# Attention tiles taken in pairs in a one-core attention, soft-MoE and SwiGLU kernel

## The chip, the cores and the metric

The kernel runs on one core of a Trainium2 chip, in one launch. Its time is device microseconds of that core; the times shown are medians of several runs. One more execution was recorded by the hardware profiler, and all durations below come from that one.

## The reference

Three stages follow each other. Eight batches with eight heads of 576 positions and 64 channels go through attention in chunks of 64 positions; the result, 4608 tokens of 512 channels, goes through a soft mixture of experts (8 experts, 4 slots each, hidden size 1024) and then through a gated feed-forward layer of 1536 channels.

```python
q_c, k_c, v_c = (a.reshape(B, H, nc, 64, D) for a in (q, k, v))
scores = scale * np.matmul(q_c, k_c.transpose(0, 1, 2, 4, 3))
attn = np.exp(scores - scores.max(-1, keepdims=True))
x = np.matmul(attn / (attn.sum(-1, keepdims=True) + 1e-9), v_c)   # as [4608, 512]
logits = x @ phi                                                  # 32 slots
d = softmax over tokens; slot_input = d.T @ x
slot_out[e] = relu(slot_input[e] @ w1[e]) @ w2[e]
y = softmax over slots of logits @ slot_out
out = (silu(y @ w_gate) * (y @ w_val)) @ w_out
```

q, k, v, phi, w1 and w2 are float32. The three weights of the last layer are float64, and the kernel turns them into pairs of float32 on the chip.

## The kernel before, in words

**Attention.** The 4608 tokens are 36 tiles of 128 (NTILE), each with 8 heads, which stand as 4 pairs of heads (j) and 2 chunks of 64 positions (cc). For tile i:

- load_qk (L293) and load_v (L296) bring q, k (512 KB) and v with a column of ones (260 KB) from HBM. Each has a ring of three buffers (NK, NV), qkbd and vbd. A load waits until the tile three before has been used: q and k by emit_scores, v by emit_pv.
- spread_k and spread_v (L321, L322) make the buffer block-diagonal: a copy of its lower 64 partitions to another place, and a memset of what they leave. They run on POOL (the first spread_k on DVE).
- emit_scores (L337): 8 small float32 matmuls into PSUM; then on DVE the row maximum (L345) and its subtraction (L347) into ssb.
- emit_pt (L359): 4 transposes of ssb against the identity, and an Exp on ACT (L361), which writes pt.
- emit_pv (L399): 8 matmuls with v, each with 130 columns, into two PSUM banks; the 65th column of each head is the row sum. DVE adds 1e-9 (L407), takes the reciprocal (L408) and multiplies (L410) into x_sb.
- emit_xt (L423): 4 transposes of x_sb, copied by ACT (L425).
- Every fourth tile, for a group g of four tiles: emit_logits (16 matmuls with phi, a running maximum, an Exp), then emit_et (one transpose of the group's weights) and emit_si (4 matmuls of 512 columns that gather the slots' inputs).

The compiler records each float32 matmul of 64 or 32 columns as two instructions in the profile, so that 8 matmuls stand there as x16.

A program order written out by hand sets what each engine does when. Each engine takes its instructions in that order and stops at one that waits. The loop (L548 to L572) for tile i is:

```python
emit_pt(i); emit_scores(i + 2); load_qk(i + 5); spread_v(i + 1); spread_k(i + 3)
emit_et; emit_xt(i - 1); emit_pv(i); load_v(i + 3); emit_logits; emit_si
if i % 2: pump(1)
```

**Weights.** All loads are issued by one queue, SP, in program order. pump takes the next entry of the list lq when one of 16 slots of 8 KB a partition (pool wp) is free: w1t and w2t are halves of an expert's weights, 1 MB each. In the attention loop it takes one entry for every two tiles; 16 halves are loaded in that way, and 4 more go into a pool (wx) that takes the place of the rings at the end. The first quarter of the gate and value weights (raw, load_gv0) is converted in steps (conv_a, conv_b, conv_c) during the attention loop, with scratch in a pool cv1.

**Experts.** emit_w1 and emit_w2 go through the experts in a fixed order; each half that has been used frees a slot (freed), and pump issues the next load.

**Feed-forward.** From L913 on the token blocks go through gate, value and output matmuls in fp32r, in an order set by SCHED; each product is split into a high and a low part (hi_sb, lo_sb), and the output takes three matmuls of 512 columns for each 128 tokens and 128 channels (L889 to L891). The output goes to HBM from SP.

**Memory.** Pools on the left side of SBUF lie one behind the other in the order in which they are opened: const, sm (small vectors, three buffers each), wp, and then those of the attention (atp, xp, xtp, cv1), whose place c_t and others take afterwards. PSUM has 8 banks: in the attention two for scores (ps_s), two for emit_pv (ps_x) and four (ps_t) for everything else.

Of the kernel before, what the change touches and what calls it, by code (L numbers as in the profile page):

```python
# [25 lines left out]
LATE = 3  # L26
C_AT = (3, 4, 5, 6, 7, 9, 10, 11, 12)
# [6 lines left out]
def tile_attn_softmoe_swiglu(  # L34
# [26 lines left out]
    cvp = [None]  # L61
    wp = ctx.enter_context(tc.tile_pool(name="wp", bufs=NW))
# [70 lines left out]
    lq = [(load_gv0, 0)]  # L133
# [42 lines left out]
    def conv_a():  # L176
# [6 lines left out]
        if c == 0 and kind != "o" and u == 1:  # L183
            i = "gv".index(kind)
            mt = tmp_t[0][:, i * 512:(i + 1) * 512]
            ex = tmp_t[0][:, 1024 + i * 256:1280 + i * 256].bitcast(U16)
        else:
            ex = cv.tile([128, 512], U16, tag="ex", name="ex", bufs=1 if cv is cv1 else 3)
            mt = cv.tile([128, 512], I32, tag="mt", name="mt")
# [13 lines left out]
    def conv_c():  # L203
# [4 lines left out]
        if c == 0 and kind != "o":  # L208
# [4 lines left out]
            if kind == "v":  # L213
                if u == 0:
                    freed(load_gv0, 0)
                else:
                    freed(alloc_tmp)
# [56 lines left out]
    with tc.manual_schedule():  # L274
        p1 = ExitStack()
        atp = p1.enter_context(tc.tile_pool(name="atp", bufs=2))
        xp = p1.enter_context(tc.tile_pool(name="xp", bufs=6))
        xtp = p1.enter_context(tc.tile_pool(name="xtp", bufs=4))
        cv1 = cvp[0] = p1.enter_context(tc.tile_pool(name="cv1", bufs=1))
        ps_s = p1.enter_context(tc.tile_pool(name="ps_s", bufs=2, space=PSUM))  # L280
        ps_x = p1.enter_context(tc.tile_pool(name="ps_x", bufs=1, space=PSUM))
        ps_t = p1.enter_context(tc.tile_pool(name="ps_t", bufs=4, space=PSUM))
# [83 lines left out]
        def emit_pv_last(i):  # L366
            pt = pt_t.pop(i)
            x = xp.tile([128, 2, 4, D], F32, tag="x", name="x_sb")
            rec = sm.tile([128, 2, 4, 1], F32, tag="rec", name="rec")
            xvs = []  # L370
            for b in range(2):
                xps = ps_s.tile([128, 512], F32, tag="s", name="x_ps")
                for j in (2 * b, 2 * b + 1):
                    for cc in range(2):
                        nc.tensor.matmul(
                            out=xps[64 * cc:64 * cc + 64, (j % 2) * 2 * VW:(j % 2 + 1) * 2 * VW],
                            lhsT=pt[:, j, 64 * cc:64 * cc + 64],
                            rhs=v_bd[i % NV][:, :, cc, j, :],
                            start=True, stop=True,
                        )  # L380
                xvs.append(xps[:, 0:4 * VW].rearrange("p (h d) -> p h d", d=VW))
            for b in range(2):
                nc.vector.tensor_scalar(
                    out=rec[:, b], in0=xvs[b][:, :, D:VW], scalar1=1e-9, scalar2=None, op0=ALU.add
                )
            for b in range(2):
                nc.vector.reciprocal(out=rec[:, b], in_=rec[:, b])
            for b in range(2):
                nc.vector.tensor_tensor(
                    out=x[:, b], in0=xvs[b][:, :, 0:D], in1=rec[:, b].to_broadcast([128, 4, D]), op=ALU.mult  # L390
                )
            x_t[i] = x.rearrange("p b h d -> p (b h d)")

        def emit_pv(i):
            pt = pt_t.pop(i)
            xps = ps_x.tile([128, 2, 512], F32, tag="x", name="x_ps")
            for j in range(4):
                for cc in range(2):
                    nc.tensor.matmul(  # L399
                        out=xps[64 * cc:64 * cc + 64, j // 2, (j % 2) * 2 * VW:(j % 2 + 1) * 2 * VW],  # L400
                        lhsT=pt[:, j, 64 * cc:64 * cc + 64],
                        rhs=v_bd[i % NV][:, :, cc, j, :],
                        start=True, stop=True,
                    )
            xv = xps[:, :, 0:4 * VW].rearrange("p b (h d) -> p b h d", d=VW)
            rec = sm.tile([128, 2, 4, 1], F32, tag="rec", name="rec")
            nc.vector.tensor_scalar(out=rec, in0=xv[:, :, :, D:VW], scalar1=1e-9, scalar2=None, op0=ALU.add)  # L407
            nc.vector.reciprocal(out=rec, in_=rec)  # L408
            x = xp.tile([128, 2, 4, D], F32, tag="x", name="x_sb")
            nc.vector.tensor_tensor(  # L410
                out=x, in0=xv[:, :, :, 0:D], in1=rec.to_broadcast([128, 2, 4, D]), op=ALU.mult
            )
            x_t[i] = x.rearrange("p b h d -> p (b h d)")
# [21 lines left out]
        def emit_logits(g, jts=(0, 1, 2, 3), done=True):  # L435
# [21 lines left out]
            et = atp.tile([128, 128], F32, tag="et", name="et")  # L457
# [14 lines left out]
        def emit_et(g):  # L472
# [3 lines left out]
            e = atp.tile([128, 128], F32, tag="e", name="e")  # L476
# [64 lines left out]
        spread_k(1)  # L541
        spread_v(0)
        spread_k(2)
        emit_scores(0)
        load_qk(3)
        emit_scores(1)
        load_qk(4)
        for i in range(NTILE - 2):  # L548
            emit_pt(i)
            emit_scores(i + 2)  # L550
            if i + 2 + NK < NTILE:
                load_qk(i + 2 + NK)
            spread_v(i + 1)
            if i + 3 < NTILE:
                spread_k(i + 3)
            if i >= 5 and (i - 5) % 4 == 0:
                emit_et((i - 5) // 4)
            if i >= 1:
                emit_xt(i - 1)
            emit_pv(i)  # L560
            if i + NV < NTILE:
# [446 lines left out]
```

## Time and profile before

| what | value |
|---|---|
| median of 3 runs | 576.01 us (574.79 to 576.03) |
| the profiled execution's own time | 579.36 us |
| its span in the profile | 577.6 us |
| TensorE (PE) busy, share of the span | 547.5 us, 95% |
| DVE, ACT, POOL busy | 422.8, 264.7, 291.6 us |
| read from HBM, written | 80.95 MB, 9.44 MB |
| chain that ended last: PE, DMA, POOL, DVE | 77%, 10%, 5%, 4% |

The profile's time is in microseconds from the span's start. The attention loop runs from about 10 us to 151 us, the experts from 160 us to about 202 us, the feed-forward layer from there to the end. In a row of the page's issues the columns are the tensors (out, from where), the queue, the count, the size and the median time from issue to landing. In the chain each row has a start, a duration and what it was: the chain is followed back from the end, at each step to what released it. A busy PE is not a PE at its peak: each matmul's recorded time covers its way through the array, and several are under way at once; the distance from one block's first start to the next block's first start tells what a block costs. The granted TensorE clock is 1.00 (2.4 GHz) in all stretches.

### The profile page before, as it was taken

The numbers are of one execution on the slowest core, as the hardware profiler recorded it, in microseconds if no ns is written. First come the engines' busy times: TensorE is split into PE (matmuls) and PEld (weight loads), VectorE is DVE, ScalarE is ACT, GpSimd is POOL, SyncE is SP. The second block draws the span as 40 slices with busy tenths as digits, with TensorE's granted clock in tenths as the row PEclk, the third lists the DMA queues.
The fourth block names the chain that finished last, engine by engine and source line by source line (L and its number), as shares of the span: only waits on it lengthen the run. The fifth ranks groups of instructions, "written<-read, shape, count | busy, mean of one in ns | idle before, by whom it ended". The sixth has DMA issues, their size and how long they took to land.

```text
span 577.6 us, 10084 instructions
## 1 busy us (share of the span) xinstructions
PE 547.5 (95%) x3823; PEld 422.4 (73%) x3823; DVE 422.8 (73%) x748; ACT 264.7 (46%) x500; POOL 291.6 (50%) x322
## 2 busy tenths in 40 slices
PE   4999999989999977999999999999999999999997
PEld 3766776776743465788888878887888788888885
DVE  4778777767566489998889887997989764443464
ACT  1344333333334467666666555564555543333331
POOL 4557654554200136667566565763766463443432
PEclk9999999999999999999999999999999999999999
DMA  8898999998989990101120221023000000032145
GB/s 274 270 333 326 313 335 325 348 320 283 350 307 385 381 393 35 36 38 30 44 74 0 74 77 70 1 74 145 1 1 1 0 2 0 14 120 87 73 177 188
DMA packets 37967, 91.03 MB, mean 158 GB/s; under 512 B 3104, under 2 KB 5152, under 8 KB 37920
## 3 DMA queue, kind: packets, MB, share of 16 engines
q1 hardware_dynamic: 37920, 90.40, 44.1%
q8 instruction: 30, 0.49, 0.3%
q14 instruction: 17, 0.14, 0.1%
HBM read 80.95 MB, written 9.44 MB: 157 GB/s over the span
## 4 chain that ended last, share of the span: by engine, by line
PE 77%; DMA 10%; POOL 5%; DVE 4%; issue 2%; ACT 1%; SPq 0%; POOLq 0%; DVEq 0%; ACTq 0%
PE o L889 16%; PE o L891 16%; PE o L890 16%; DMA vbd<-in_v_dram 7%; PE v_ps L845 4%; PE s_ps L337 4%; PE g_ps L845 4%; PE x_ps L399 4%; PE h_ps L648 3%; DMA w2t<-in_moe_w_dram 2%; PE xt_ps L423 2%; PE gg_ps L826 2%; PE so_ps L693 1%; PE pt_ps L359 1%; PE si_ps L488 1%
## 5 line engine op out<-in xcount | busy, mean ns | idle before, releaser
L858 POOL TENSOR_TENSOR lo_sb<-s_sb,hi_sb 128x512 fp32r<-128x512 f32 x106 | 140.6, 1327 | 134.0 <-ACT hi_sb L857 130.8
L889 PE MATMUL o<-whl,hi_sb 128*128 128x512 f32 x428 | 167.4, 391 | 3.8 <-DVE part L898 3.8
L891 PE MATMUL o<-whl,lo_sb 128*128 128x512 f32 x428 | 166.8, 390 | 0.5 <-POOL lo_sb L858 0.5
L890 PE MATMUL o<-whl,hi_sb 128*128 128x512 f32 x428 | 166.7, 390 | 0.0
L848 ACT ACTIVATE s_sb<-g_ps 128x512 f32<-128x512 f32 (+1 forms) x110 | 64.7, 590 | 153.2 <-PE g_ps L845 151.0
L849 DVE TENSOR_TENSOR s_sb<-s_sb,v_ps 128x512 f32<-128x512 f32 (+1 forms) x110 | 73.9, 673 | 77.8 <-ACT s_sb L848 76.4
L889 PEld LDWEIGHTS o<-whl,hi_sb 128*128 128x128 f32 x428 | 80.3, 188 | 23.6 <-DVE part L898 5.9
L891 PEld LDWEIGHTS o<-whl,lo_sb 128*128 128x128 f32 x428 | 80.3, 188 | 17.7 <-POOL lo_sb L858 0.9
L890 PEld LDWEIGHTS o<-whl,hi_sb 128*128 128x128 f32 x428 | 80.4, 188 | 16.2
L857 ACT ACTIVATE hi_sb<-s_sb 128x512 fp32r<-128x512 f32 (+1 forms) x110 | 67.6, 616 | 0.8 <-DVE s_sb L849 0.8
L902 DVE TENSOR_TENSOR part<-part,o 128x512 f32<-128x512 f32 x92 | 57.0, 676 | 2.6 <-PE o L891 2.6
L337 PE MATMUL s_ps<-qkbd 128*64 128x128 f32 x576 | 42.0, 291 | 15.4 <-POOL qkbd L322 9.6
L219 POOL TENSOR_TENSOR mt<-mt,ex 128x512 f32<-128x512 f32 x32 | 39.5, 1234 | 30.6 <-PE g_ps L845 15.1
L337 PEld LDWEIGHTS s_ps<-qkbd 128*64 128x64 f32 x576 | 32.9, 144 | 22.4 <-POOL qkbd L322 12.4
L205 DVE SCALAR_TENSOR_TENSOR ex<-raw,ex 128x512 uint16<-128x512 uint16 x34 | 49.1, 1443 | 0.1
L321 POOL COPY vbd<-vbd 64x520 f32<-64x520 f32 x36 | 22.8, 632 | 48.9 <-DMA vbd<-in_v_dram 46.5
L845 PE MATMUL v_ps<-c_t,g_st 128*128 128x512 f32 (+1 forms) x110 | 42.6, 391 | 3.1 <-ACT s_sb L848 2.5
L345 DVE TENSOR_REDUCE m<-s_ps 128x8 f32<-128x512 f32 x36 | 24.8, 690 | 26.4 <-PE s_ps L337 26.4
L845 PE MATMUL g_ps<-c_t,g_st 128*128 128x512 f32 (+1 forms) x110 | 42.2, 386 | 0.1
L361 ACT ACTIVATE pt<-pt_ps 128x512 f32<-128x512 f32 x36 | 21.3, 594 | 45.8 <-PE pt_ps L359 45.8
L399 PE MATMUL x_ps<-vbd,pt 128*64 128x130 f32 x560 | 39.0, 280 | 0.0
L200 DVE SCALAR_TENSOR_TENSOR mt<-mt,raw 128x512 f32<-128x512 f32 x34 | 36.1, 1063 | 0.0
(144 smaller groups left out, 721.2 us busy)
## 6 DMA issues: line engine op xcount, KB each, us to landing
qkbd<-in_qk_dram SPq DMA_DIRECT2D x36, 512.0 KB, 5.9
w1t<-in_moe_w_dram SPq DMA_DIRECT2D x16, 1024.0 KB, 8.0
w2t<-in_moe_w_dram SPq DMA_DIRECT2D x15, 1024.0 KB, 10.6
vbd<-in_v_dram SPq DMA_DIRECT2D x36, 260.0 KB, 5.4
out_dram<-part SPq DMA_DIRECT2D x36, 256.0 KB, 2.1
raw<-in_moe_w_out_dram SPq DMA_DIRECT2D x6, 1024.0 KB, 7.6
raw<-in_moe_w_gate_dram SPq DMA_DIRECT2D x5, 1024.0 KB, 5.4
raw<-in_moe_w_val_dram SPq DMA_DIRECT2D x5, 1024.0 KB, 5.1
```

The costliest lines, as they stand in the source:

```text
L205: nc.vector.scalar_tensor_tensor(out=ex, in0=hh, scalar=0x8000, in1=ex, op0=ALU.bitwise_and, op1=ALU.bitwise_or)
L337: nc.tensor.matmul(out=sp[64 * cc:64 * cc + 64, j, :], lhsT=qk_bd[i % NK][:, 0, j, t0:t0 + 64], rhs=qk_bd[i % NK][:, 1:3, j, t0:t0 + 64], ...
L399: nc.tensor.matmul(out=xps[64 * cc:64 * cc + 64, j // 2, (j % 2) * 2 * VW:(j % 2 + 1) * 2 * VW], lhsT=pt[:, j, 64 * cc:64 * cc + 64], rhs= ...
L845: nc.tensor.matmul(out=ps[:, k], lhsT=g_st[:, c, gi, ff:ff + 128], rhs=c_blk(b)[:, k], start=True, stop=True)
L848: nc.scalar.activation(out=s[:, k], in_=gp[:, k], func=ACTF.Silu)
L849: nc.vector.tensor_tensor(out=s[:, k], in0=s[:, k], in1=vp[:, k], op=ALU.mult)
L857: nc.scalar.activation(out=hi[:, k], in_=s[:, k], func=ACTF.Copy)
L858: eng.tensor_tensor(out=lo[:, k], in0=s[:, k], in1=hi[:, k].bitcast(F32), op=ALU.subtract)
L889: nc.tensor.matmul(out=a, lhsT=hi[:, ts], rhs=w_hi, start=first, stop=False)
L890: nc.tensor.matmul(out=a, lhsT=hi[:, ts], rhs=w_lo, start=False, stop=False)
L891: nc.tensor.matmul(out=a, lhsT=lo[:, ts], rhs=w_hi, start=False, stop=last)
L902: nc.vector.tensor_tensor(out=p[:, t], in0=p[:, t], in1=a, op=ALU.add)
```

## The change

The attention loop takes two tiles per step. emit_pv takes a pair p (tiles 2p and 2p+1): its 16 matmuls fill three PSUM banks, with three products of 130 columns in a bank instead of two (xa has two banks, xb one), and the DVE work is done once for the 12 heads of xa and once for the 4 heads of xb, six instructions for two tiles as before. load_v for tiles 2p+3 and 2p+4 is called inside emit_pv, after each tile's matmuls. emit_pv_last goes. Scores, transposes and spreads of two tiles stand next to each other. PSUM is now 2 banks for scores, 3 for emit_pv and 3 for the rest (4 before).

The pool cv1 goes: the first conversions use a slot of wp as scratch (alloc_tmp at the head of lq), which is freed after the second one. xp has 4 buffers of two tiles instead of 6 of one, et and e one buffer each. The strip pad_l of 416 bytes opens the pool const; rec in the pool sm grows from 8 to 16 floats, three times, which is 96 bytes. Both together move wp and all that lies behind it on that side by 512 bytes; the constants behind the strip move by 416.

```diff
+    const.tile([128, 104], F32, name="pad_l")
...
-    lq = [(load_gv0, 0)]
+    lq = [(load_gv0, 0), (alloc_tmp,)]
...
-        if c == 0 and kind != "o" and u == 1:
+        if c == 0 and kind != "o":
...
-        xp = p1.enter_context(tc.tile_pool(name="xp", bufs=6))
+        xp = p1.enter_context(tc.tile_pool(name="xp", bufs=4))
-        cv1 = cvp[0] = p1.enter_context(tc.tile_pool(name="cv1", bufs=1))
-        ps_t = p1.enter_context(tc.tile_pool(name="ps_t", bufs=4, space=PSUM))
+        ps_t = p1.enter_context(tc.tile_pool(name="ps_t", bufs=3, space=PSUM))
...
+        def emit_pv(p):
+            xa = ps_x.tile([128, 2, 512], F32, tag="xa", name="xa_ps")
+            xb = ps_x.tile([128, 512], F32, tag="xb", name="xb_ps")
+            banks = [xa[:, 0], xa[:, 1], xb]
+            for n in range(8):
+                i, j = 2 * p + n // 4, n % 4
+                for cc in range(2):
                     nc.tensor.matmul(
+                        out=banks[n // 3][64 * cc:64 * cc + 64, (n % 3) * 2 * VW:(n % 3 + 1) * 2 * VW],
+                        lhsT=pt_t[i][:, j, 64 * cc:64 * cc + 64],
                         rhs=v_bd[i % NV][:, :, cc, j, :],
                         start=True, stop=True,
                     )
+                if j == 3:
+                    pt_t.pop(i)
+                    if i + NV < NTILE:
+                        load_v(i + NV)
...
-        for i in range(NTILE - 2):
-            emit_pt(i)
-            emit_scores(i + 2)
...
+        NP = NTILE // 2
+        for p in range(NP):
+            if p < NP - 1:
+                for i in (2 * p + 2, 2 * p + 3):
+                    emit_scores(i)
+                    if i + NK < NTILE:
+                        load_qk(i + NK)
+            emit_pv(p)
+            for i in range(2 * p + 2, min(2 * p + 4, NTILE)):
+                if i + 2 < NTILE:
+                    spread_k(i + 2)
+                spread_v(i)
+            if p >= 3 and p % 2:
+                emit_et((p - 3) // 2)
+            if p >= 1:
+                emit_xt(2 * p - 2)
+                emit_xt(2 * p - 1)
+            if p < NP - 1:
+                emit_pt(2 * p + 2)
+                emit_pt(2 * p + 3)
+            if p >= 2 and p % 2 == 0:
+                emit_logits(p // 2 - 1)
+            if p >= 3 and p % 2:
+                if p == NP - 1:
+                    emit_logits(NG - 1, (0, 1), False)
+                emit_si((p - 3) // 2)
+            pump(1)
+            conv_step(p >= CV_FROM and conv_pos() < 2 and not conv_busy())
```

**PE, four tiles in the middle of the loop.** Before (s_ps scores, pt_ps and xt_ps transposes, x_ps the products with v, lt_ps logits, e_ps and si_ps the group's work; qkbd and vbd are the rings; x4 and x8 are matmuls of one row):

```order
23 L359 MATMUL pt_ps<-ident,ssb 128x128 x4
24 L337 MATMUL s_ps<-qkbd_101 64x128 x8
25 L475 MATMUL e_ps<-ident,et 128x128
26 L423 MATMUL xt_ps<-ident,x_sb 128x128 x4
27 L399 MATMUL x_ps<-vbd_105,pt 64x130 x8
28 L488 MATMUL si_ps<-x_sb,e 32x512 x4
29 L359 MATMUL pt_ps<-ident,ssb 128x128 x4
30 L337 MATMUL s_ps<-qkbd_102 64x128 x8
31 L423 MATMUL xt_ps<-ident,x_sb 128x128 x4
32 L399 MATMUL x_ps<-vbd_103,pt 64x130 x8
33 L359 MATMUL pt_ps<-ident,ssb 128x128 x4
34 L337 MATMUL s_ps<-qkbd_100 64x128 x8
```

and now:

```order
23 L359 MATMUL pt_ps<-ident,ssb 128x128 x8
24 L428 MATMUL lt_ps<-xt,phi_sb 32x128 x16
25 L337 MATMUL s_ps<-qkbd_100 64x128 x8
26 L337 MATMUL s_ps<-qkbd_98 64x128 x8
27 L373 MATMUL xa_ps<-vbd_101,pt 64x130 x8
28 L373 MATMUL xa_ps<-vbd_102,pt 64x130 x4
29 L373 MATMUL xb_ps<-vbd_102,pt 64x130 x4
30 L462 MATMUL e_ps<-ident,et 128x128
31 L410 MATMUL xt_ps<-ident,x_sb 128x128 x8
32 L359 MATMUL pt_ps<-ident,ssb 128x128 x8
33 L475 MATMUL si_ps<-x_sb,e 32x512 x4
34 L337 MATMUL s_ps<-qkbd_99 64x128 x8
```

The shape changed 18 times in four tiles; it now changes 8 times, and the transposes of x_sb and of ssb stand in one run.

**SP, the load queue, two pairs in the middle of the loop.** Before:

```order
31 L293 DMA qkbd_101<-in_qk_dram 128x1024
32 L296 DMA vbd_105<-in_v_dram 128x520
33 L293 DMA qkbd_102<-in_qk_dram 128x1024
34 L296 DMA vbd_103<-in_v_dram 128x520
35 L88 DMA w1t<-in_moe_w_dram 128x2x1024
36 L293 DMA qkbd_100<-in_qk_dram 128x1024
```

and now:

```order
30 L293 DMA qkbd_99<-in_qk_dram 128x1024
31 L293 DMA qkbd_100<-in_qk_dram 128x1024
32 L296 DMA vbd_103<-in_v_dram 128x520
33 L296 DMA vbd_101<-in_v_dram 128x520
34 L90 DMA w1t<-in_moe_w_dram 128x2x1024
35 L293 DMA qkbd_98<-in_qk_dram 128x1024
```

The same five loads per pair, with both of q and k ahead of both of v. On POOL spreads of k and v alternate as before, and the four of a step now stand together (qkbd and vbd are the rings' buffers):

```order
52 L321 COPY qkbd_98<-qkbd_98 64x512
53 L322 MEMSET qkbd_98 64x512
54 L321 COPY vbd_102<-vbd_102 64x520
55 L322 MEMSET vbd_102 64x520
56 L321 COPY qkbd_99<-qkbd_99 64x512
57 L322 MEMSET qkbd_99 64x512
58 L321 COPY vbd_103<-vbd_103 64x520
59 L322 MEMSET vbd_103 64x520
```

These eight rows are one step of the new loop, for the tiles 2p+4, 2p+2, 2p+5 and 2p+3. Each copy waits for its own load, and what stands behind it on POOL waits with it, as before.

## Rows read from the trace of the kernel before

**Rows 1.** Busy time by stretch: attention, its steady part, experts, loads alone; first row columns.

```profile
core 0: us, PE busy (x) PEld busy (x) DVE busy (x) ACT busy (x) POOL busy (x), PEclk, DMA share, GB/s
14.80:148.90 134.10, 126.57 (x1676) 94.70 (x1672) 99.99 (x224) 49.14 (x103) 75.64 (x134) 1.00 0.92 318
...
64.06:144.08 80.02, 75.78 (x1006) 56.45 (x1006) 57.60 (x130) 27.68 (x60) 44.02 (x81) 1.00 0.93 322
...
160.30:198.50 38.20, 37.34 (x312) 14.28 (x312) 24.71 (x98) 17.29 (x36) 2.74 (x10) 1.00 0.97 352
170.00:190.00 20.00, 20.00 (x173) 8.33 (x166) 13.88 (x59) 8.85 (x21) 0.50 (x4) 1.00 1.05 383
```

**Rows 2.** Chain that ended last, one stall of the attention loop; start, duration, what.

```profile
79.56 1.09 PE s_ps L337 x16
...
85.57 1.06 PE x_ps L399 x16
86.65 6.61 DMA vbd<-in_v_dram
93.39 0.62 POOL vbd L321
94.06 0.53 POOL vbd L322
94.59 0.56 POOL qkbd L321
95.20 0.53 POOL qkbd L322
95.78 1.09 PE s_ps L337 x16
```

**Rows 3.** Timeline of PE, one tile without a stall; start, duration, line, operation.

```profile
18.09 1.11 PE L399 MATMUL x_ps<-vbd,pt 128*64 128x130 f32 x16
...
19.12 0.66 PE L359 MATMUL pt_ps<-ident,ssb 128*128 128x128 f32 x4
...
19.71 1.09 PE L337 MATMUL s_ps<-qkbd 128*64 128x128 f32 x16
...
20.74 0.66 PE L423 MATMUL xt_ps<-ident,x_sb 128*128 128x128 f32 x4
...
21.32 1.11 PE L399 MATMUL x_ps<-vbd,pt 128*64 128x130 f32 x16
...
22.36 0.66 PE L359 MATMUL pt_ps<-ident,ssb 128*128 128x128 f32 x4
```

**Rows 4.** Timeline of PE at the end of attention, where two blocks of one shape touch.

```profile
146.84 1.09 PE L359 MATMUL pt_ps<-ident,ssb 128*128 128x128 f32 x8
147.86 1.06 PE L488 MATMUL si_ps<-x_sb,e 128*32 128x512 f32 x8
148.85 1.11 PE L399 MATMUL x_ps<-vbd,pt 128*64 128x130 f32 x16
149.79 1.05 PE L375 MATMUL x_ps<-vbd,pt 128*64 128x130 f32 x16
```

**Rows 5.** Page, DMA issues: the three kinds of load in the attention loop.

```profile
qkbd<-in_qk_dram SPq DMA_DIRECT2D x36, 512.0 KB, 5.9
w1t<-in_moe_w_dram SPq DMA_DIRECT2D x16, 1024.0 KB, 8.0
...
vbd<-in_v_dram SPq DMA_DIRECT2D x36, 260.0 KB, 5.4
```

**Rows 6.** Groups by line, 60 to 140 us: busy, mean ns, idle before, releaser.

```profile
L337 PE MATMUL s_ps<-qkbd 128*64 128x128 f32 x320 | 22.1, 279 | 4.5 <-POOL qkbd L322 4.5
...
L425 ACT ACTIVATE xt<-xt_ps 128x512 f32<-128x512 f32 x20 | 11.9, 597 | 16.2 <-PE xt_ps L423 16.2
...
L441 PE MATMUL lt_ps<-xt,phi_sb 128*32 128x128 f32 x160 | 5.4, 276 | 0.0
```

**Rows 7.** Chain that ended last, experts: their first matmuls and the last load.

```profile
160.31 1.92 PE h_ps L648 x16
...
186.65 11.72 DMA w2t<-in_moe_w_dram
```

More of the change, by code (lines that the diff above doesn't have):

```diff
@@ L26 @@
 LATE = 3
+CV_FROM = 3
 C_AT = (3, 4, 5, 6, 7, 9, 10, 11, 12)
@@ L404, in emit_pv @@
                     )
[L405 to L409, printed above, removed]
+                if j == 3:
+                    pt_t.pop(i)
+                    if i + NV < NTILE:
+                        load_v(i + NV)
+            x = xp.tile([128, 2, 512], F32, tag="x", name="x_sb")
+            rec = sm.tile([128, 16, 1], F32, tag="rec", name="rec")
+            av = xa[:, :, 0:6 * VW].rearrange("p b (h d) -> p b h d", d=VW)
+            bv = xb[:, 0:4 * VW].rearrange("p (h d) -> p h d", d=VW)
+            ra, rb = rec[:, 0:12].rearrange("p (b h) o -> p b h o", b=2), rec[:, 12:16]
+            xv = x.rearrange("p t (h d) -> p (t h) d", d=D)
+            nc.vector.tensor_scalar(out=ra, in0=av[:, :, :, D:VW], scalar1=1e-9, scalar2=None, op0=ALU.add)
+            nc.vector.reciprocal(out=ra, in_=ra)
             nc.vector.tensor_tensor(
-                out=x, in0=xv[:, :, :, 0:D], in1=rec.to_broadcast([128, 2, 4, D]), op=ALU.mult
-            )
-            x_t[i] = x.rearrange("p b h d -> p (b h d)")
+                out=xv[:, 0:12].rearrange("p (b h) d -> p b h d", b=2), in0=av[:, :, :, 0:D],
+                in1=ra.to_broadcast([128, 2, 6, D]), op=ALU.mult,
+            )
+            nc.vector.tensor_scalar(out=rb, in0=bv[:, :, D:VW], scalar1=1e-9, scalar2=None, op0=ALU.add)
+            nc.vector.reciprocal(out=rb, in_=rb)
+            nc.vector.tensor_tensor(
+                out=xv[:, 12:16], in0=bv[:, :, 0:D], in1=rb.to_broadcast([128, 4, D]), op=ALU.mult
+            )
+            x_t[2 * p], x_t[2 * p + 1] = x[:, 0], x[:, 1]
         xt_t = {}
@@ L475, in emit_et @@
             nc.tensor.transpose(ps[:, 0:128], et, ident)
-            e = atp.tile([128, 128], F32, tag="e", name="e")
+            e = atp.tile([128, 128], F32, tag="e", name="e", bufs=1)
             nc.scalar.activation(out=e, in_=ps[:, 0:128], func=ACTF.Copy)
@@ L573, in tile_attn_softmoe_swiglu @@
-        spread_v(NTILE - 1)
+        spread_v(1)
+        for i in range(2):
+            emit_scores(i)
+            load_qk(i + NK)
+        spread_k(3)
+        for i in range(2):
+            emit_pt(i)
+        NP = NTILE // 2
+        for p in range(NP):
+            if p < NP - 1:
+                for i in (2 * p + 2, 2 * p + 3):
+                    emit_scores(i)
+                    if i + NK < NTILE:
+                        load_qk(i + NK)
+            emit_pv(p)
[19 more added lines that the diff above has]
+            conv_step(p >= CV_FROM and conv_pos() < 2 and not conv_busy())
```

80 lines of the change are left out of this document (8 added, 72 removed).

## The prediction

> **What bounds the kernel now.** I read the busy times by stretch first, then the chain that ended last, then single blocks on PE. From the first products with v to those of tile 34, attention takes 134.1 us [rows 1]: 34 tiles, or 8.5 groups of four at 15.8 us. In the steady part five groups take 80.0 us, 16.0 each. PE and the DMA engines are both close to full there: 75.8 us of 80 for PE, and a DMA share of 0.93. The loads move 322 GB/s in that stretch, though 383 GB/s at a share of 1.05 in the experts [rows 1].
>
> What a group costs PE is read from distances between block starts. One tile goes from 18.09 to 21.32, 3.23 us: products 1.03, transposes of ssb 0.59, scores 1.03, transposes of x 0.58 [rows 3]. Four tiles are 12.9; the gathering matmuls add 0.99 [rows 4], the logits about 1.0 (5.4 us of five groups, rows overlapping at their ends) [rows 6], the one transpose of the group's weights about 0.2. That is 15.1 us of work in a period of 16.0.
>
> The missing 0.9 is one stall per group, and the chain names it. Products end at 86.6; only then is a buffer of v free; its load lands 6.61 later; POOL spreads this v and only then the k that stands behind it in POOL's order; the scores of that k start at 95.78 [rows 2]. So a load of v holds up scores that do not read it. The idle time before scores, 4.5 us from 60 to 140 us, has POOL's last memset as its releaser [rows 6]; 0.9 per group again.
>
> After attention nothing is gained or lost by this stretch's order: the first expert matmul starts at 160.31, which frees slots for the remaining loads, and the last of those lands at 198.4 [rows 7] after a stretch with a DMA share of 0.97 [rows 1]. What the attention saves shifts everything behind it.
>
> **The change, part by part.**
>
> *Fewer changes of shape on PE.* Where two blocks of one shape touch already, eight transposes take 1.02 (146.84 to 147.86) against 2 x 0.59 = 1.18, which saves 0.16; the second of two product blocks starts 0.94 after the first (148.85 to 149.79) and not 1.03, which saves 0.09 [rows 3, 4]. The order changes shape 18 times in four tiles before and 8 times after. Ten fewer at 0.09 to 0.16 are 0.9 to 1.6 us; I take 0.13, near the middle, since both kinds of block are joined equally often. PE's work falls from 15.1 to 13.8 us per group.
>
> A page of the Trainium skill bears on this: "TensorEngine Tiling (Array Packing)", Key Properties, says that a change of the tiling mode drains TensorE. Scores and products both use 64 columns, so by that rule the step between them, which the new order has twice a group, costs nothing: 12 changes go and not 10, and PE would need 13.5. No block of the trace has scores directly before products without a wait, so the rows do not show it; the sum below keeps 13.8.
>
> *The loads.* A group moves the same bytes: 4 x (524 + 266) + 2 x 1049 KB = 5.26 MB. At 383 GB/s that is 13.7 us, at 322 it is 16.3 [rows 1]. The engines' own busy time lies between: 0.93 x 16.0 = 14.9 us per group, if packets take as long as now. They took longer per byte than in the experts, where many loads are always queued. In the new order two of q and k and two of v follow each other, so the queue should run dry less often, but nothing in the trace shows that mix.
>
> *The rings.* Still three buffers each. Scores of tile 2p+2 free the buffer that tile 2p+5 needs one step later, at the same place of the step. The load takes 5.9 us in the median [rows 5], the spread 95.73 less 94.59 = 1.1 [rows 2], the handovers some 0.3: a step of at least 7.3 us, 14.6 per group. For v it is 5.4 + 1.2 + 0.3 = 6.9, 13.8 per group. The old chain, in which scores wait for a v that they don't read, has 2T - 3 us in the new order for the same 6.6 + 2.4, with T a step; at any T over 6.1 it does not stall.
>
> So three limits stand close together: PE 13.8, rings 14.6, DMA 14.9. None is strictly periodic, and a landing that is late by a microsecond stops PE, so the real value lies a little above the largest: **15.0 us per group**, with 13.8 (PE alone) and 16.3 (loads at 322 GB/s) as ends. The stretch becomes 8.5 x 15.0 = 127.5 us: **-6.6**.
>
> *Start.* The first products now wait until the scores of tile 3 are done and two v are spread. That is at most one tile later, +3.2, and at best nothing; the next steps then already save, and I take +0.5.
>
> *End.* The last two product blocks touched already; two transposes and the scores join: -0.4. The gathering of the seventh group moves behind the last products, with its 1.0 inside the sum on both sides.
>
> *PSUM.* Three buffers for transposes, not four. Within a run of four blocks of 0.44 the fourth waits for ACT's copy of the first, 0.6 us [rows 6], that starts when that block is done: it is free at about 1.3, as the fourth is due. Nothing to 0.6 a step; covered by the slack that PE has against the loads (15.0 - 13.8 = 1.2 per group), so 0; without that cover 17 x 0.6 = 10 us at the worst.
>
> *DVE, POOL, ACT.* The same element counts, so DVE keeps its 57.6 us of 80, POOL its 44.0, ACT its 27.7 [rows 1]; six DVE instructions per pair remain six. Nothing. Conversion: the same 14 instructions in the same loop, with scratch elsewhere. Its slot is taken from the weights until the second conversion is done, but only one load is drawn per pair, and 16 halves are drawn by the end of attention in both orders, the last about a pair later. The experts' loads have (1.05 - 0.97) x 38.2 = 3 us of room [rows 1] for that; if it were gone, one half of 1 MB costs 2.7.
>
> *The strip.* 3 x 32 more bytes in rec and 416 in the strip are 512, so whatever lies behind them keeps its address modulo 512. The constants move by 416. The products with v read buffers at three different residues (each is 4160 bytes, 64 over a multiple of 512) and take 1.03 and 1.04 in consecutive tiles [rows 3]; so I count nothing for the constants. No row shows fp32r operands at another residue.
>
> **Sum.** -6.6 + 0.5 - 0.4 = -6.5 us. The profiled execution's own 579.4 would become 572.9. It lies 3.4 above the median of the runs, 576.0, and against that I forecast **569.5 us**.
>
> **The rivals.**
>
> *PE alone sets the pace.* If a queue that never runs dry brings the loads to 383 GB/s, and landings with it below 5.5 us, a group takes 13.8: 8.5 x 2.0 = -17 us, **559**. For it: the 383 of the experts. Against it: the rings' 7.3 us a step. Chance 0.20. By the Trainium skill's rule on tiling modes it would be 13.5 a group, 556.5; that does not move the forecast, which PE does not set.
>
> *The loads stay as slow as they are.* At 322 GB/s a group takes 16.0 to 16.3 whatever PE needs, and the time stays at 574 to 577, **576**. For it: the share of 0.93 is already high. Against it: a stall per group that POOL's order explains, and PE's 15.1. Chance 0.15. The Trainium skill's "Perfetto Trace Analysis", Optimization Strategy, would speak for it: a gap that repeats can mean too few buffers, and the rings stay at three.
>
> *Loads in bunches land too late, and the kernel gets slower.* Each step now asks for 2.6 MB within some 3 us, so k can land behind a weight half. The step is landing + 1.4; it decides at 8.0 us a step, the pace of now, or a landing of 6.6, which the row of the chain has for v. At 7.0 the group takes 16.8: +8.5 us, **584**. For it: weights take 8.0 in the median [rows 5]. Against it: both q and k are asked for early in a step, and at a slower pace the queue empties. Chance 0.12.
>
> *The strip does not do what it says.* If later operands stood at another residue and that mattered, the feed-forward layer would change; the arithmetic above excludes a move. Chance 0.03, either way slower.
>
> **How the numbers follow.** The forecast with 14.4 to 15.6 a group, 564 to 574.5, has 0.50. All differences up to 0.3% (1.7 us) are about what a measurement of this kernel can tell from no change. Faster by more: 0.50 + 0.20 and 0.02 of the third case, 0.72. Within: 0.14. Slower: 0.14. The range of 8 in 10 reaches from the PE-bound side, **560**, to just over no change, **577**; outside lie some 0.05 below and 0.13 above.
>
> **What would show it.** In the profile after: attention from first products to tile 34's in 127.5 us; blocks of 16 transposes and 16 products without a gap; a DMA share near 1.0 with 340 to 355 GB/s there; PE's idle time before scores or products ended by POOL behind a load. Wrong would be: a DMA share under 0.9 with PE full (first rival), 322 GB/s and 16.0 again (second), landings of q and k over 6.6 us (third), a feed-forward layer that takes longer from its first output matmul to the end.

## The result, and the profile after

The changed kernel takes **568.82 us** in the median of 4 runs (567.59 to 570.47); the kernel before, on the same chip, 576.02. The ratio is **0.9864** (95% interval 0.9839 to 0.9888): 7.2 us faster. The profiled execution took 570.47 us with a span of 568.5; both profiled executions lie above their medians, so the spans differ by 9.1 and the medians by 7.2. Stages are compared by the spans. Each span is one execution: in the six profiled kernels with this same attention code (this one, e2, e5, e6, e10 and e13 below) the first expert matmul stands between 148.7 and 153.2 us, so a difference of 2 us between two stages tells little by itself.

| starts, us | before | after | difference of the stage that it begins |
|---|---|---|---|
| first scores | 5.83 | 5.83 | +3.8 (8.8 to 12.6) |
| first products with v | 14.61 | 18.43 | -16.2 (134.2 to 118.1) |
| products of tile 34 | 148.85 | 136.50 | +3.1 (11.5 to 14.5) |
| first expert matmul | 160.31 | 151.02 | 0.0 (43.5) |
| first gate matmul | 203.85 | 194.53 | +0.2 (373.70 to 373.95) |
| end of the span | 577.55 | 568.48 | |

Everything happened in the attention. The rows that answer to [rows 1], busy time by stretch with the same columns (attention; five groups from one gathering to the one five later; experts):

```profile
core 0: us, PE busy (x) PEld busy (x) DVE busy (x) ACT busy (x) POOL busy (x), PEclk, DMA share, GB/s
18.43:136.50 118.07, 112.75 (x1644) 93.72 (x1640) 94.01 (x218) 42.74 (x97) 73.39 (x129) 1.00 0.96 346
57.12:128.76 71.64, 69.35 (x1006) 57.13 (x1005) 58.15 (x137) 26.41 (x63) 46.71 (x82) 1.00 0.99 367
151.02:189.20 38.18, 37.36 (x315) 14.31 (x316) 24.72 (x98) 17.30 (x36) 2.74 (x10) 1.00 0.98 352
```

Five groups take 71.64 us, 14.33 each, where the kernel before took 80.02, or 16.0 [rows 1]. The loads went from 322 to 367 GB/s, and the experts moved ahead unchanged.

PE's work is read from the timeline of the changed kernel, one group; start, duration, line, operation, idle time before and what ended it:

```profile
57.12 1.06 PE L475 MATMUL si_ps<-x_sb,e 128*32 128x512 f32 x8
58.11 1.97 PE L337 MATMUL s_ps<-qkbd 128*64 128x128 f32 x32
59.91 1.50 PE L373 MATMUL xa_ps<-vbd,pt 128*64 128x130 f32 x24
61.24 0.61 PE L373 MATMUL xb_ps<-vbd,pt 128*64 128x130 f32 x8
61.78 1.09 PE L410 MATMUL xt_ps<-ident,x_sb 128*128 128x128 f32 x8
62.71 1.07 PE L359 MATMUL pt_ps<-ident,ssb 128*128 128x128 f32 x8
63.71 1.08 PE L428 MATMUL lt_ps<-xt,phi_sb 128*32 128x128 f32 x32
64.72 1.09 PE L337 MATMUL s_ps<-qkbd 128*64 128x128 f32 x16
66.56 1.09 PE L337 MATMUL s_ps<-qkbd 128*64 128x128 f32 x16 [0.75 <-POOL qkbd L322]
```

Two blocks of scores take 1.80 where [rows 3] has 2 x 1.03, two of products 1.87 against 2 x 1.03, four of transposes 1.93 against 4 x 0.59. The shortest distances between such blocks in the loop (scores 1.797, products 1.332 and 0.542, transposes 0.873 and 1.00, each twice; logits 1.011, gathering 0.995, the group's transpose 0.165) add up to **13.26 us** a group. That is a lower bound; the period is 14.33, so up to 1.07 of stall is left.

The stall changed its place. In the chain that ended last it stood in v alone [rows 2]; now, from 18 to 137 us, it has four loads of v and four of q and k (pieces cut with ...):

```profile
61.01 6.24 DMA vbd<-in_v_dram
...
67.37 0.62 POOL vbd L321
68.04 0.54 POOL vbd L322
...
68.62 0.67 PE xa_ps L373 x8
...
82.91 5.78 DMA vbd<-in_v_dram
...
95.22 6.04 DMA qkbd<-in_qk_dram
```

The row that answers to [rows 6] agrees. By groups of lines, 57.12 to 128.76 us (busy, mean ns, idle before, releaser), scores wait 1.8 us in five groups, not 4.5:

```profile
L337 PE MATMUL s_ps<-qkbd 128*64 128x128 f32 x320 | 20.6, 277 | 1.8 <-POOL qkbd L322 1.8
L373 PE MATMUL xa_ps<-vbd,pt 128*64 128x130 f32 x240 | 16.8, 277 | 0.5 <-POOL vbd L322 0.5
```

The landings of [rows 5] hardly moved, on the page of the changed kernel:

```profile
qkbd<-in_qk_dram SPq DMA_DIRECT2D x36, 512.0 KB, 5.7
w1t<-in_moe_w_dram SPq DMA_DIRECT2D x16, 1024.0 KB, 8.1
...
vbd<-in_v_dram SPq DMA_DIRECT2D x36, 260.0 KB, 5.5
```

**The start** gives 3.8 us back. Timeline of PE after:

```profile
10.49 1.97 PE L337 MATMUL s_ps<-qkbd 128*64 128x128 f32 x16 [2.69 <-POOL qkbd L322]
12.39 1.12 PE L359 MATMUL pt_ps<-ident,ssb 128*128 128x128 f32 x4
13.98 1.11 PE L359 MATMUL pt_ps<-ident,ssb 128*128 128x128 f32 x4 [0.47 <-DVE ssb L347]
15.02 3.58 PE L337 MATMUL s_ps<-qkbd 128*64 128x128 f32 x32
18.43 1.50 PE L373 MATMUL xa_ps<-vbd,pt 128*64 128x130 f32 x24
```

Transposes of tile 1 and scores of tile 3 now stand ahead of the first products: 1.6 us of work, which left the stretch behind. But here each block takes about twice as long as in the loop (32 scores 3.58 against 1.97). The granted clock cannot be read there. The trace's clock record begins only at 18.36 us, just where the full pace begins (at 15.2 us in the kernel before), and the 1.00 printed for a stretch ahead of it is not a measurement; what the section on the profile before says of the clock holds from 15.2 us on. At this pace the two cost 2.8; a wait for ssb and a spread of k that ended 0.6 later make up the rest.

**The end** gives 3.1 back. One tile's transposes, the group's transpose and the gathering of group 7 (0.5 + 0.2 + 1.0) moved behind the products of tile 34; the other 1.4 is new waiting, part of which the timeline names:

```profile
139.88 1.44 PE L428 MATMUL lt_ps<-xt,phi_sb 128*32 128x128 f32 x15 [0.25 <-ACT xt L412]
...
143.15 0.90 PE L410 MATMUL xt_ps<-ident,x_sb 128*128 128x128 f32 x4 [0.29 <-DVE acc L486]
```

Without the moved work (1.6 + 1.7) the stretch became 12.9 us shorter and not 16.2; start and end cost 2.2 and 1.4. That is 12.9 / 8.5 = 1.5 us a group, from 15.8 to 14.3.

### The profile page after: what moved, and what is told of

Same layout as the page of the kernel before. It is cut to its first block, busy times and chain, and to the rows that moved or that the text cites. A ratio compares the mean times of both kernels' runs of the same rounds, so it can differ in the third digit from the quotient of the medians.

```text
span 568.5 us, 10116 instructions
## 1 busy us (share of the span) xinstructions
PE 540.1 (95%) x3823; PEld 425.8 (75%) x3823; DVE 419.2 (74%) x745; ACT 260.6 (46%) x500; POOL 292.1 (51%) x322
## 4 chain that ended last, share of the span: by engine, by line
PE 80%; DMA 12%; DVE 4%; POOL 2%; issue 1%; ACT 1%; SPq 0%; POOLq 0%; DVEq 0%; ACTq 0%
PE o L877 17%; PE o L879 17%; PE o L878 17%; DMA qkbd<-in_qk_dram 5%; PE v_ps L833 4%; DMA vbd<-in_v_dram 4%; PE g_ps L833 4%; PE s_ps L337 4%; PE xa_ps L373 3%; PE h_ps L636 3%; DMA w2t<-in_moe_w_dram 2%; PE gg_ps L814 2%; PE pt_ps L359 2%; PE xt_ps L410 2%; PE so_ps L681 1%; PE lt_ps L428 1%
## 5 line engine op out<-in xcount | busy, mean ns | idle before, releaser
L220 POOL TENSOR_TENSOR mt<-mt,ex 128x512 f32<-128x512 f32 x32 | 39.6, 1237 | 30.5 <-PE g_ps L833 14.4
L337 PE MATMUL s_ps<-qkbd 128*64 128x128 f32 x576 | 40.5, 293 | 12.3 <-POOL qkbd L322 6.5
L207 DVE SCALAR_TENSOR_TENSOR ex<-raw,ex 128x512 uint16<-128x512 uint16 x32 | 47.7, 1490 | 0.1
L412 ACT ACTIVATE xt<-xt_ps 128x512 f32<-128x512 f32 (+1 forms) x36 | 19.4, 589 | 47.7 <-PE xt_ps L410 47.6
L321 POOL COPY qkbd<-qkbd 64x512 f32<-64x512 f32 x35 | 21.4, 612 | 30.5 <-DMA qkbd<-in_qk_dram 27.4
L202 DVE SCALAR_TENSOR_TENSOR mt<-mt,raw 128x512 f32<-128x512 f32 x32 | 34.6, 1081 | 0.0
L194 DVE TENSOR_SCALAR mt<-raw 128x512 int32<-128x512 int32 x32 | 32.9, 1027 | 0.0
```

What stands on the lines that cost most here:

```text
L207: nc.vector.scalar_tensor_tensor(out=ex, in0=hh, scalar=0x8000, in1=ex, op0=ALU.bitwise_and, op1=ALU.bitwise_or)
L220: nc.gpsimd.tensor_tensor(out=m, in0=m, in1=p, op=ALU.mult)
L337: nc.tensor.matmul(out=sp[64 * cc:64 * cc + 64, j, :], lhsT=qk_bd[i % NK][:, 0, j, t0:t0 + 64], rhs=qk_bd[i % NK][:, 1:3, j, t0:t0 + 64], ...
```

## The experiments

Four questions: what the order of the spreads is worth and what the joined shapes, what holds the loop now, whether the start can be won back, and what the strip does. A ratio is to the kernel before on the same chip.

### The order on POOL alone: e1_k_before_v

My theory was that scores wait for a v that they do not read. The kernel before, with the spread of k put ahead of that of v and nothing else:

```diff
-            spread_v(i + 1)
             if i + 3 < NTILE:
                 spread_k(i + 3)
+            spread_v(i + 1)
```

> The kernel before, with the two spreads of a loop step swapped on POOL: spread_k of tile i+3 ahead of spread_v of tile i+1, nothing else. Theory A (the stall of 0.9 us per group comes from POOL's order, where a late v holds back the k behind it): the stall goes, a group takes 15.1 us instead of 16.0 to 16.2, and the time falls by 8.5 x 0.9 = 7 to 8 us to about 568.5. Rival B (the loads' rate sets the pace at a DMA share of 0.93): the stall moves to the products' wait for v or to the loads, a group stays at 16, and the time stays within 2 us of 576.

Measured: 571.70 us, ratio **0.9893** (0.9868 to 0.9917). Its busy times over five groups and its scores (by stretch, then by line, 64.39 to 141.05 us):

```profile
64.39:141.05 76.66, 76.39 (x1015) 57.33 (x1013) 58.51 (x133) 28.21 (x61) 43.07 (x79) 1.00 0.96 339
```

```profile
L337 PE MATMUL s_ps<-qkbd 128*64 128x128 f32 x320 | 21.9, 279 | 0.3 <-POOL qkbd L322 0.3
```

The time falls by 6.8 us, a little less than the 7 to 8 of theory A (the 568.5 in it was for another chip). The wait for k falls from 4.5 us [rows 6] to 0.3, and five of the six groups from 34.3 to 125.0 us take exactly 15.06 us, which is PE's work in tile order (15.1 in the prediction). The stall of the kernel before was the order on POOL. Swapping two statements gives 1.07% where the whole change gives 1.36% (the intervals overlap).

### The pairs without joined shapes: e3_shapes_apart

The changed kernel with its loads, spreads and PSUM, but PE's blocks of a pair placed apart:

```diff
+            for h in range(2):
+                i = 2 * p + 2 + h
...
+                    emit_scores(i)
...
+                if p >= 1:
+                    emit_xt(2 * p - 2 + h)
+                emit_pv_mm(p, range(4 * h, 4 * h + 4))
+                if p < NP - 1 and h == 0:
+                    emit_pt(i)
+            emit_pv_dve(p)
```

> The changed kernel with PE's blocks taken apart again: scores, transposes of x, products and transposes of ssb of one tile, then of the other; the loads, POOL's and DVE's work of a pair, PSUM and the rings stay as in the change. Theory A (joined shapes are the gain: PE's work per group fell from 15.1 to 13.3 us and the stall of about 1 us stayed): PE's work returns to about 15 us, a group takes 15.8 to 16.2 instead of 14.3, and the time rises by 8.5 x 1.5 to 1.9 = 13 to 16 us to 582 to 585. Rival B (the order of loads and spreads is the gain): a group stays near 14.5 to 15.1, PE's work being hidden in the old stall, and the time at 570 to 575.

Measured: 584.58 us, ratio **1.0113** (1.0088 to 1.0139). From first to last products it takes 137.1 us, the changed kernel 119.8. PE's shortest distances add up to 15.1 us a group again, 1.9 more than joined, and 1.9 x 8.5 = 16 of the 17.3 us. But it is not a pure measure, and that the two numbers meet is partly luck: the changed kernel's stall is gone and another has taken its place. Between 44.47 and 111.23 us four groups take 15.6 to 17.5, and the transposes of ssb wait for DVE (by groups of lines):

```profile
L359 PE MATMUL pt_ps<-ident,ssb 128*128 128x128 f32 x65 | 10.2, 277 | 6.1 <-DVE ssb L347 6.1
```

The chain that ended last runs mostly through DVE there: subtractions, the division of the products, a conversion. So e3 shows that the new order of loads and spreads does not pay with the blocks placed in this way. That loads in pairs gain nothing by themselves is not shown. What the joined shapes are worth is seen better in two kernels in which PE hardly waits: 15.06 us a group in e1 and 13.49 in e9, the next run.

### What holds the loop now: e9_no_weights_in_loop, e7_four_k_rings, e8_fifteen_slots

PE needs at least 13.26 us a group and gets 14.33. Either a ring of three is too short, or the transfers are too slow. In e9 the weights stay out of the loop (they are asked for after it, so its total time, 596.87 us in one execution, tells nothing):

```diff
-            pump(1)
+            if p < 2:
+                pump(1)
```

> The changed kernel with the weight halves left out of the attention loop (they are asked for only after it, so the experts wait some 40 us for them; only the attention is read). Theory A (the rings' own latency sets the stall): landings of q, k and v stay at 5 us or more, and five groups take 70 to 72 us. Theory B (the transfers compete for the rate): landings fall under 4.5 us, the stalls of 5.5 to 6.6 us in the chain disappear, and five groups take the 13.3 us of PE each, 66 to 68 us.

Five groups of e9, by stretch, and its landings in that stretch:

```profile
53.58:121.02 67.44, 67.30 (x1007) 57.30 (x1006) 58.18 (x138) 26.57 (x63) 48.05 (x83) 1.00 0.70 233
```

```profile
qkbd<-in_qk_dram SPq DMA_DIRECT2D x19, 512.0 KB, 4.3
vbd<-in_v_dram SPq DMA_DIRECT2D x20, 260.0 KB, 4.8
```

A group takes 13.49, and PE stands 0.14 us of 67.44. With the same rings of three the stall is gone as soon as the weights are. So the weights' transfers make the stall, as theory B has it, although v lands in 4.8 and not under 4.5.

In e7 a fourth buffer for q and k is paid for with one weight slot; e8 gives up the slot alone:

```diff
-NW = 16
+NW = 15
...
-        NK, NV = 3, 3
+        NK, NV = 4, 3
...
+        load_qk(3)
```

> The changed kernel with four buffers for q and k instead of three (v keeps three), paid for with one weight slot of sixteen. Theory A: the stall of about 1.07 us that is left per group of four tiles (14.33 less 13.26 of work on PE) comes from the rings, a buffer that is asked for only one step ahead; then the half of the stalls in which scores wait for q and k go, five groups from si to si take 67 to 70 us instead of 71.6, and the kernel is 3 to 5 us faster than the control with fifteen slots. Theory B: the loads' rate is the limit (DMA share 0.99 there); then the wait only moves to the loads of v, five groups stay at 71 to 72.5 us with the share at 0.98 to 1.00, and both kernels agree within 1.7 us.

> The control: the changed kernel with fifteen weight slots instead of sixteen, rings of three. Theories A and B alike: attention as in the changed kernel, 71 to 72.5 us for five groups; one slot fewer may delay one half of weights in the experts, 0 to 2.7 us more in all (568 to 573).

Measured: e7 570.86 us, 0.9874 (0.9827 to 0.9920); e8 572.54 us, 0.9930 (0.9901 to 0.9959). Five groups of each by stretch, e7 and then e8:

```profile
56.02:127.56 71.54, 68.14 (x1006) 57.25 (x1006) 58.06 (x138) 26.46 (x63) 46.35 (x83) 1.00 0.98 362
```

```profile
56.91:128.01 71.10, 69.09 (x1006) 57.17 (x1006) 59.25 (x139) 26.43 (x63) 47.16 (x82) 1.00 1.00 372
```

The fourth buffer gains nothing in the loop. The scores' wait is gone, but the products now wait for v, whose ring still has three buffers (e7, by groups of lines, the same five groups):

```profile
L375 PE MATMUL xa_ps<-vbd,pt 128*64 128x130 f32 x240 | 16.5, 276 | 3.4 <-POOL vbd L324 3.4
```

Two readings are left. One is the rate: 5.25 MB a group take 14.2 to 14.3 us at 362 to 372 GB/s with a share of 0.98 to 1.00. The other is a ring of three with the landings that this traffic makes: 5.8 for q and k and 5.7 for v in e7's loop are a step of about 7.2 by the prediction's own sum, 14.4 a group. e9 fits both, since its landings are short. Four buffers for q and k and for v at once would tell them apart; no run has them. At the 383 GB/s of [rows 1] the bytes of a group would take 13.7 us.

The missing slot shows in the experts, 46.8 us in e8 and 45.7 in e7 instead of 43.5; that this is more than the 2.7 that I allowed is a small miss.

### The start: e4_warm_start, e11_early_weights, e13_changed_again

e4 puts 12 matmuls of the identity ahead of the first scores and 22 behind them, to see whether the slow pace at the start costs time:

```diff
+        warm(12)
         for i in range(2):
             emit_scores(i)
             load_qk(i + NK)
+            if i == 0:
+                warm(22)
```

> The changed kernel with 12 matmuls of the identity ahead of the first scores and 22 between the first and the second; they compute nothing that is used. Theory A (the first blocks run at half pace because PE was idle: 16 scores take 1.97 us there and 1.09 later): the blocks from the second scores to the first products take half as long, the first products start at about 15.5 to 16 instead of 18.4 us, and the time falls by 2 to 3 us to about 566. Rival B (the start is set by the loads and spreads of the third and fourth k): first products at 18 us or later and less than 0.7 us gained.

Measured: 570.14 us, 0.9865 (0.9841 to 0.9890), as the changed kernel. The first 16 scores take 1.09 and not 1.97, and the first products start at 17.29 instead of 18.43 (timeline of PE):

```profile
6.09 1.09 PE L337 MATMUL s_ps<-qkbd 128*64 128x128 f32 x16
...
17.29 1.50 PE L373 MATMUL xa_ps<-vbd,pt 128*64 128x130 f32 x24
```

That start lies between the two theories. By the first expert matmul 0.2 us of it is left (150.8 against 151.0), as rival B has it for the time: PE's pace at the start does not bound the attention.

e11 uses the idle transfers there (share 0.26 from 14 to 18 us), and e13 is its control:

```diff
             load_qk(i + NK)
+        pump(3)
         spread_k(3)
```

> The changed kernel with the loop's first three loads (the second half of the first gate and value columns, a slot of scratch, one half of expert weights) asked for as soon as the scores of the second tile are out, where the DMA engines idle (share 0.26 at 14 to 18 us). Nothing else moves. Theory A (the transfers' rate bounds attention, so an idle stretch of the engines is lost time): the halves of the loop are drawn three steps earlier, all slots are full before the loop's end, its last groups take 13.3 to 13.8 us, and the kernel is 1.5 to 4 us faster than the changed kernel. Theory B (the early loads only push the next q and k back): the first products stand 1 to 3 us later and the time is the same within 1.7 us.

> The changed kernel as it is, on the chip of this set, as the control of the one with early weights: 0.984 to 0.989 of the kernel before.

Measured: e11 572.77 us, 0.9904 (0.9869 to 0.9940); e13 570.34 us, 0.9871 (0.9833 to 0.9909). Both theories missed: the share from 14 to 18 us rises to 0.98, the first products stay at 18.23, and the kernel is, if anything, 2.4 us slower (the intervals overlap). In e11 the loss stands in the second step. Timeline, then clock and share by stretch:

```profile
21.13 1.09 PE L337 MATMUL s_ps<-qkbd 128*64 128x128 f32 x16
24.23 1.53 PE L337 MATMUL s_ps<-qkbd 128*64 128x128 f32 x16 [2.00 <-POOL qkbd L322]
25.54 2.78 PE L373 MATMUL xa_ps<-vbd,pt 128*64 128x130 f32 x24
```

```profile
21.00:24.00 3.00, 1.23 (x18) 0.85 (x16) 2.27 (x6) 0.95 (x2) 0.96 (x2) 1.00 1.01 366
24.00:27.00 3.00, 2.77 (x30) 2.77 (x32) 1.17 (x2) 0.00 (x0) 1.63 (x4) 0.62 1.03 413
```

The early weights push the q and k of tile 5 back, PE waits 2.0 us, and after a stretch in which it was busy for 1.23 of 3.00 us the granted clock falls: 0.62 in the mean of the next, and 0.50 (1.2 GHz, its lower level) from 24.73 to 28.14; the products take 2.6 instead of 1.33. (e13 waits there too, 1.4 us for v, and keeps its clock.) Nor does the head start come back later: the last group is bound by PE in both (12.3 and 12.2 us), and the slots are full before attention ends (share 0.70 from 128 to 150 us, 0.94 in e13). No version that I ran is clearly faster than the changed kernel.

### The strip: e2_no_strip, e6_strip_32_bytes, e5_strip_384_bytes, e10_right_side_moved

The fp32r matmuls of the feed-forward layer have their moving operands (whl, c_t) on the left side of the memory, behind the strip, and their stationary ones (hi_sb, lo_sb, g_st) on the right side, at 480 mod 512. No trace shows an address; these places, and those below, are my own account of the pools' layout. What the runs surely change is the shift: the strip has 416, 384, 32 or no bytes, and e10 moves the right side by 64. e2 takes the strip away, which puts the left side at 64 mod 512 and the constants back where the kernel before had them:

```diff
-    const.tile([128, 104], F32, name="pad_l")
```

> The changed kernel without the strip of 416 bytes: everything behind it lies 416 bytes lower, so that the fp32r weights and the tokens' coefficients stand at 64 modulo 512 and the constants where they were before. Theory A (addresses do not matter to the pace): 568.8 within 1 us, and the output matmuls keep their 391 ns and their distance. Rival B (fp32r operands at another residue are read more slowly): attention and experts as in the changed kernel, and the feed-forward layer, some 350 us of matmuls, longer by 1% to 5%: 572 to 586 us.

Measured: 579.10 us, ratio **1.0008** (0.9990 to 1.0026): the whole gain is gone. Of the 10.6 us between the two spans 8.4 are in the layer; the other 2.2 are in the attention of the one profiled execution, the slowest of e2's twelve (581.09). By stretch from first gate matmul to the end, after and e2:

```profile
194.53:568.48 373.95, 362.44 (x1629) 297.31 (x1628) 284.56 (x384) 192.64 (x348) 204.14 (x155) 0.99 0.19 66
```

```profile
196.76:579.11 382.35, 369.75 (x1629) 296.53 (x1628) 286.38 (x384) 191.28 (x348) 203.66 (x155) 1.00 0.18 65
```

The changed kernel's 0.99 is a short fall of its clock (0.66 in the mean of 215 to 220 us); e2 is at 1.00, so the clock does not make e2 slower. The 8.4 us are spread over all fp32r matmuls of 512 columns. Groups of lines from 205 us on, after and e2:

```profile
L878 PE MATMUL o<-whl,hi_sb 128*128 128x512 f32 x428 | 167.1, 391 | 0.0
```

```profile
L877 PE MATMUL o<-whl,hi_sb 128*128 128x512 f32 x418 | 165.0, 395 | 0.0
```

4 to 5 ns each on 1284 output matmuls and 220 for gate and value make 6 to 7.5 of the 8.4. It is not the constants: before and e2 have them in the same place, and their layers differ by 8.6.

Three more places, in one execution each, ask what makes one fast: 96 and 448 mod 512 for the left side, and 416 for the right side with the left at 480. The edit

```diff
-    const.tile([128, 104], F32, name="pad_l")
+    const.tile([128, 8], F32, name="pad_l")
```

is e6; e5 has 96 in the place of 104, and e10 keeps 104 and adds

```diff
+        padr = ctx.enter_context(tc.tile_pool(name="padr", bufs=1, side="right"))
+        padr.tile([128, 16], F32, name="pad_r")
```

> The changed kernel with a strip of 32 bytes instead of 416: the moving fp32r operands of the feed-forward layer lie at 96 mod 512 instead of 480 (64 without a strip), the stationary ones stay at 480. Theory A: only an equal place of both operands modulo 512 is fast; then the layer takes 382 us as without a strip, 8.5 more than with 416 bytes. Theory B: what counts is the place modulo 64 (480 and 96 are both 32 over a multiple, 64 is none); then the layer takes 373.5 to 374.5 us as in the changed kernel. Anything between the two speaks for a gradual effect of the distance.

> The changed kernel with a strip of 384 bytes: the moving fp32r operands of the feed-forward layer at 448 mod 512, the stationary ones still at 480. Theory A (only an equal place of both is fast): the layer takes 381 to 383 us. Theory B (the distance counts gradually: 32 here, 96 and 128 in the two slow cases): it takes 375 to 378 us. Theory C (a place near the end of 512 bytes is fast, whatever the other operand does): 373.5 to 374.5 us.

> The changed kernel with its strip of 416 bytes, so that the moving operands lie at 480 mod 512, and 64 bytes more on the other side of the memory, so that the stationary operands (and the vector results beside them) lie at 416. Theory A (an equal place of both operands is what is fast): the layer takes 381 to 383 us. Theory C (the moving operand's own place at 480 is what is fast): 373.5 to 374.5 us, as in the changed kernel.

The layer by stretch, e6, e5 and e10:

```profile
192.30:573.81 381.51, 368.87 (x1629) 297.02 (x1628) 286.10 (x384) 191.44 (x348) 203.77 (x155) 1.00 0.18 65
```

```profile
192.10:574.38 382.28, 370.91 (x1629) 297.82 (x1628) 286.63 (x384) 191.40 (x348) 203.68 (x155) 1.00 0.18 65
```

```profile
194.10:573.08 378.98, 367.51 (x1629) 298.17 (x1628) 285.58 (x384) 192.49 (x348) 204.39 (x155) 1.00 0.19 65
```

Neither a place modulo 64 nor a distance decides: 96 and 448 are as slow as 64. e10 is slow as well, by 5.0, so the moving operand's own place is not all; but it is less than the 381 to 383 of theory A. What stands: in the ten profiled kernels with both sides at 480 the layer took 373.4 to 374.6 us, in the four where the sides differ 379.0 to 382.4; the smallest gap, 4.4 us, is over three times the spread of the ten. Whether it is their difference or each side's place that counts, and by what mechanism, stays open; no run moved both sides together.

## Why the prediction was right, point by point

The forecast was 569.5 us in 560 to 577, faster with 0.72. Measured: 568.82. The sign, the cause and the range were right. That the number came within 0.7 us is partly luck. The terms were off by more than that and cancelled: the loop gave 12.9 us and not 6.6, start and end took 3.6 and not 0.1. And the spans of the profiled executions differ by 9.1 us, not by the 6.5 of the forecast; the medians differ by 7.2 because the kernel before was profiled 3.3 above its median and the changed one 1.7.

- **The stall.** "A load of v holds up scores that do not read it": shown by e1, where the wait fell from 4.5 to 0.3 us in five groups.
- **PE's work**, 15.1 to 13.8 a group: the mechanism was right, the size off. It is 13.26 by shortest distances (13.49 in e9), and 1.8 us for the joined blocks lies beyond the 1.6 that was the end of my range. The rule of the Trainium skill, "TensorEngine Tiling (Array Packing)", Key Properties, has two more of the changes of shape cost nothing (13.5); the rows agree with it: 32 scores directly ahead of products take 1.80, 0.90 for each 16, against 1.03 ahead of another shape [rows 3]. I kept 13.8 for want of a row, but the row was there: in the kernel before, the scores that start at 12.84 us stand directly ahead of products at 14.61 without a wait, 1.77 us, and those of 9.89 take 1.91 ahead of transposes at 11.80, at the same slow pace of the start.
- **The loads**, 14.9 as a share of 0.93 x 16.0 "if packets take as long as now": this condition failed. 0.99 x 14.33 = 14.2 us of busy time move the same 5.25 MB a group. I had named a queue that runs dry as what may make packets slow, and then not priced it. e1, with a share of 0.96 at 339 GB/s, lies between the two kernels. The traces' records of packets speak against it for v: over five groups each, its packets of 2080 bytes took 108 ns in the mean before, 107 in e1, 94 in the changed kernel and 94 in e9, whose queue is the driest (share 0.70); the median is 85 in all four. That is 512 x 14 / 16 = 0.45 of the 0.7 us a group. It goes with two loads of v standing together in the queue; why, no run shows. The packets of 4096 bytes took 180, 173 and 172 ns, and 198 in e9, where they are q and k alone; there a dry queue may be the reason.
- **The rings**, 14.6: neither shown nor excluded as the limit. Their 7.3 us a step was made with a landing that was itself a result of the full transfers (5.9; 4.3 in e9, which reaches 13.5 with rings of three). With the landings measured in the loop the same sum gives 14.4, as near to 14.33 as the transfers' 14.2; e7 deepened one ring, and the wait moved to the other.
- **The sum of the loop**: 15.0 a group became 14.3, so -6.6 became -12.9. This is the largest miss, and 14.33 lies just below the 14.4 to 15.6 that I gave the forecast's own case.
- **The start**, +0.5 within 0 to +3.2: it is +2.2 without the moved work. I had priced a tile at the loop's pace; there PE runs at half of it. Yet e4, which brings the full pace, keeps 0.2 us of the 1.1 that it wins there: start and loop are not terms of their own, as the sum has them.
- **The end**, -0.4: it is +1.4. I counted joined blocks and not new waits; the rows above name 0.25 for ACT and 0.29 for DVE, and the rest stays open.
- **The strip**, nothing: right as a difference between the two kernels (373.70 and 373.95), and the reason given, the same place modulo 512, fits e2. But "no row shows another residue" hid a price as large as the gain. e2 shows that price. The rival in which the strip fails fell, since its two sums of bytes do give 512.
- **The rivals.** PE alone (559): PE had 13.3 to give, and the loads held it at 14.3. Loads as slow as before: fell, 367 GB/s. Landings too late: 5.7 and not over 6.6. All three turned on the transfers, and e9 was the run that priced the weights among them.

## What to carry to other kernels

When a wait repeats with the loop, look first at what stands ahead of the waiting work on the engine that releases it: here the swap of two statements on POOL brought most of what a new order of the whole loop brought. A share of busy time of the DMA engines is not a constant of the bytes: compare GB/s per share of a stretch in which many loads are queued before calling it a limit. And when a pool's size changes, check the place of everything behind it; a slowdown of one per cent in every matmul of another stage does not look like a cause that lies in this one.

## What the runs showed of the hardware that I had not expected

- fp32r matmuls of 512 columns take 391 ns with both operands at 480 mod 512 (by my account of the layout) and 395 ns with the moving one at 64: 8.4 us over the layer, from 416 bytes in a pool that these matmuls do not read.
- At the start, blocks of PE take twice their time (16 scores 1.97) until the trace's clock record begins, at 18.36 us; in e4, after matmuls of the identity, it begins at 5.29 and 16 scores take 1.09. In e11, where the record has 1.2 GHz, products take twice their time as well (2.6 against 1.33). The start has the pace of the lower level, though no record has the clock there.
- The DMA engines moved 322 GB/s at a share of 0.93 in the kernel before [rows 1] and 367 at 0.99 after, with the same kinds of load: worked out to a share of 1.00, 346 and 371 GB/s.
